# Two layers of linear attention and GELU MLP on one core: the same items in another hand-written order, with f's and y's in longer runs and eleven warming products instead of twelve

## The chip, the cores and the metric

One core of a Trainium2 chip. The metric is the device time of one execution in microseconds, as the median of the runs. The engines are TensorE (PE; its weight loads are PEld), VectorE (DVE), ScalarE (ACT), GpSimd (POOL) and SyncE (SP), which issues nearly all the DMAs.

## The reference

x has 2048 rows of 448 numbers. Two layers are computed, each a linear attention and an MLP, with the same weights in both:

```python
phi = lambda t: jnp.where(t > 0, t + 1, jnp.exp(t)) + 1e-6
def _A_ref(x, wqkv, wo):                      # H = 16 heads of Dh = 28
    q, k, v = ...                             # x @ wqkv, split by heads
    pq, pk = phi(q), phi(k)
    kv = jnp.einsum("bhsd,bhse->bhde", pk, v)
    z = jnp.einsum("bhsd->bhd", pk)
    num = jnp.einsum("bhqd,bhde->bhqe", pq, kv)
    den = jnp.einsum("bhqd,bhd->bhq", pq, z)[..., None] + 1e-6
    return (num / den) @ wo
def _B_ref(x, w1, b1, w2, b2):                # F = 1792
    return gelu(x @ w1 + b1) @ w2 + b2
x = x + _A_ref(layernorm(x), wqkv, wo)
x = x + _B_ref(layernorm(x), w1, b1, w2, b2)  # and both once more
```

## The kernel before

**Tiles and precision.** The 2048 rows are 16 tiles of 128 (t = 0 to 15), in blocks of four. A float32 operand is split into a rounded part and a rest (h and l in the names, for high and low), and a product is three products: high by high, high by low, low by high. Such a split is a cast on ACT (`copy`, L227) for the high part and a subtraction on DVE or POOL for the low one. Since 448 is three pieces of 128 and a tail of 64, the tails of high and low share one piece, so that a product over 448 has 11 matmuls.

**Items.** The whole program is a list of items, two texts in the table `ORDER` (L15 to L118), one for each layer. `run`, at the end of the kernel, goes through a text and calls the function that each item names, with the number behind it as its tile or chunk. A `>` in front of an item means that it belongs to the next layer, so the first text also holds the head of layer 1; a letter behind a colon overrides an engine, a buffer or a bank. Nothing reorders the instructions afterwards: the order of the text is the order in each engine's queue, and each engine works its queue from front to back. An instruction that waits holds up all that is queued behind it on its engine.

**The items that matter here.**

- `hot12` (L240 to L244): twelve products of a 128 x 128 tile of ones with 512 columns of ones, into a bank that nobody reads.
- `ld`, `a`, `ar`, `n`: load of a tile of x on SP; its mean and variance (DVE); the inverse root (POOL); the normalised tile (DVE, or ACT).
- `tu`, `st`, `sp`: a transpose by 32 x 32 squares (DVE), its store and its reload, which put the transposed tile in place; `xh` and `xl` split it (ACT, DVE). In the start-up the transposes are TensorE's instead: `ht`, `hx`, `hl` for tiles 0 and 1, `T` for 2 and 3.
- `K` and `Q` (`proj`, L563 to L567): 11 matmuls of 448 columns each, for one tile. In the start-up the same products are written one matmul at a time, as `hk` and `hq` (L507), in the order in which the pieces of the weights arrive. `wkld`, `wkh`, `wkl`, and the same with q, load and split these weights.
- `ke` and `kp`: phi of K, two passes on ACT and one on DVE. `kh` (ACT, L596) and `kl` (DVE, L600) split it; `za` sums it over the tiles. `qe`, `qp` and `qs` are the same for Q, with a store.
- `sh` (ACT) and `sl` (POOL, L555, L556): the split of the normalised tile as it lies. `G` (L636 to L640): 11 matmuls that add the product of that tile and of phi(K) to four banks.
- `wv`, `wo`: loads of the v and o weights; `woh` and `wol` split the latter. `gt`, `z`, `zb`, `dc` close the sums; `kv` (L709) forms the heads' matrices from the copies of G (`gt`) and the v weights (tile wvt); `m` to `mc` multiply them with wo.
- `pl` to `pT`: the rows of phi(Q) come back, are divided by their denominators and transposed; `o` and `oc` multiply them with the heads' matrices, and `oa` adds the result to x.
- `bld`, `bhi`, `blo`: load (SP), cast (ACT) and subtraction (POOL) of the weights w1 (numbers below 16) and w2 (16 and up), through buffers named xn, W5 and W6; these are the loads called stg from in_B_w_dram.
- `f` (L912 to L917): for a block of four tiles, 11 matmuls of 512 columns that make one chunk of 128 of the 1792 hidden columns. n counts over 14 chunks and 4 blocks, 56 in a layer. `g` is the GELU (ACT, L922), `gh` its cast (ACT, L227), `gl` the low part (DVE, L932).
- `y` (L941 to L944): the chunk's share of the second product, 12 matmuls of 448 columns into four banks. `u` is one of y's four banks alone, written at a block's first chunk. `ya` adds the result to x, `ys` stores it.

**What limits the order.** There are eight banks: four for G and y (`acc`), two for f and Q (`h`), two for K and others (`m`). f(n) takes the bank that g(n−2) has read. The casts gh and the low parts gl have two buffers each (A and B), freed by the y that reads them, and g has three. The start-up buffers xn are two.

Of the kernel before, what the change touches and what calls it, by code (L numbers as in the profile page):

```python
# [16 lines left out]
        "ld0 a0 hot12 ar0 ld1 a1 ar1 wkld1 n0 d0 wkh1 wkld0 ht0 hx0 n1 d1 wkh0 wkl1 ht1 ht2 hl0 wkl0 ld2 wkld2 "  # L17
        "wqld1 wqld0 wkld3 wqld3 ld6 wqld2 ld3 bld4:xn ld4 ld5 hk2 ht3 hk3 hx2 hx1 hl1 wkh2 wqh1 hx3 wqh0 wkl2 "
        "a2 wql1:p wkh3 wqh3 wqh2 hk0 hk8 hk13 hk11 hk14 hk12 hk7 hk4 hk1 hl2 hl3 hq8 hk16 hk9 hq2 hk5 hq7 hq11 "
        "hk18 hq19 hk19 hq3 wkl3 hk10 hk6 wql0 wql3 hk15 hq0 hq1 wql2 hq9 hq10 hq6 hq4 hq5 ar2 ke0 sh0 a3 kp0 n2 "  # L20
        "za0 hq21 hq14 hk17 hq18 hq16 hk20 hq13 hq12 hk21 hq15 hq20 hq17 qe0 kh0 d2 qp0 T2 ar3 sl0 n3 kl0 a5 G0 "
        "ke1 xh2 sh1 ar5 sl1 kp1 xl2 a4 kh1 bld3:xn bhi3 d3 bhi4 qe1 ar4 K2 n5 kl1 n4 tu4 tu5 T3 G1 ld10 qs0 ld9 "
        "ld7 st2 ke2 sh3 qp1 xh3 kp2 a6 za1 a7 xl3 Q2 K3 blo4 sl3 blo3 bld6:xn qs1 ld11 bld2:xn sp2 ar7 ar6 n7 "
        "a9 n6 kh2 sh2 ar9 sl2 kl2 tu6 za2 Q3 bhi2 G2 bhi6 ke3 xh4 tu7 kp3 za3 xh5 kh3 blo2 blo6 ld8 ld14 "
        "bld8:xn st3 bld9:xn xl4 K4 qe3 bhi8 ke4 qe2 xl5 kl3 n9 qp3 K5 Q4 G3 a8 kp4 blo8 ar8 n8 a11 bhi9 kh4 ke5 "
        "sh4 za4 blo9 sl4 ar11 tu9 a14 ar14 kl4 G4 sp3 kp5 xh7 za5 kh5 xh6 bias1:a qs3 bld11:xn ld15 wo0 n14 sh5 "
        "qp2 xl6 tu8 a10 K6 sl5 Q5 qe4 sh6 qp4 n11 kl5 G5 ke6 sl6 ar10 kp6 n10 xl7 bld5:xn bhi5 ld12 st4 qs4 "
        "ld13 sp4 tu14 tu10 tu11 Q7 K7 kh6 bhi11 qe5 xh8 a12 qp5 a13 kl6 blo11 blo5 ar12 za6 ar13 st5 qs2 "
# [12 lines left out]
        "Q13:acc Q12:acc Q14:m mu2 mu3 qe15 qe10 pd5 pz4 pc4 pd4 pm4 pz6 blo24 pc6 qp15 pd6 ld5 ms1 mp0 mp1 yh0 "
        "yh1 bhi25 yl1 pu4 qp10 yl0 yh3 yh2 yl2 yl3 qs15 qs9 bld13:xn qs10 qe13 qe12 bhi13 pl7 pz7 blo13 pc7 pm5 "
        "f0 g0 pu5 gh0 qp13 gl0 pd7 ps2 pm7 pm6 pu6 f1 f2 g1 gh1 qp12 u2 u3 f3 u0 u1 bld19:xn pl9 pz9 pc9 gl1 "
        "pd9 mc2 mc3 qs12 pl8 g2 gh2 g3 pm9 pu9 gl2 y1 gh3 qe11 pz8 qp11 lb3 lb0 pc8 qe14:W6 pd8 gl3 mc0 mc4 "
        "bld21:xn pl10 bhi19 blo19 mc1 pp2 ld7 qs13 lb1 pu7 pz10 blo25 pc10 pd10 bhi21 mc5 ld6 qs11 mc7 pl11 ld9 "
        "bld29:W5 pz11 blo21 mc6 pl13 ps3 bld22:xn pp3 bld23:xn f6 f4 g4 g6 y2 y3 gh4 f5 f9 g5 qh4 bhi22 gh5 "
        "bhi29 gl4 qp14 y4 f7 qh5 gh6 ql4 gl5 g7 ql5 pm8 pm10 oc4 oc5 f8 g9 bhi23 pc11 blo22 blo29 pu10 qh6 ql6 "
        "pu8 gl6 qs14 >wqld0 oa5 oa4 qh7 ps4 bld27:W5 bld26:W6 bhi26 pp4 oc6 y5 y6 gh7 g8 >tab0 gh9 qh8 la4 ar4 "
        "lb2 ln4 pd11 blo23 gl7 la5 ql7 oc7 pz13 pc13 oa6 la6 y7 gl9 qh9 ar6 ln6 ql9 oc9 gh8 gl8 y8 y9 f10 g10 "
        "pm11 mu4 f12 tab1 g12 ar5 blo26 oa7 ln5 f11 mu5 la7 pu11 bld28:W6 pl14 ms2 bhi27 g11 ar7 pd13 oa9 la9 "  # L50
        "ar9 lb6 pl15 ln7 lb7 blo27 mu6 mu7 ql8 mp2 ps5 ms3 pp5 mp3 f13 gh11 pz14 pc14 pd14 gl11 oc8 yh4 g13 "
        "gh10 gl10 y10 y11 yh5 gh12 bhi28 yh7 blo28 gh13 yh6 yl4 yl5 pm13 gl12 yl7 y12 gl13 y13 lb4 pz15 ya0 "
# [960 lines left out]
```

## Time and profile before

| | us |
|---|---|
| median of 3 runs | 870.22 (868.93 to 870.95) |
| the profiled execution | 869.59 |
| its span, from the first to the last recorded instruction | 867.8 |
| PE busy | 860.4 |
| DVE, ACT, POOL busy | 452.7, 356.5, 214.4 |
| the twelve hots, start and length | 1.06, 5.49 |
| start of the first f of layer 0 | 134.05 |
| start of the first f of layer 1 | 561.74 |

A row of the timeline gives the start, the length, the engine and line, the operation, what it writes and reads, the shape, and how many like rows it stands for; in brackets, if the engine was idle before, for how long and what it waited for. A length is that of one matmul through the array; since matmuls overlap, their price is read from one start to the next.

### The profile page before, as it was taken

The numbers are of one execution on the slowest core, as the hardware profiler recorded it, in microseconds if no ns is written. First come the engines' busy times: TensorE is split into PE (matmuls) and PEld (weight loads), VectorE is DVE, ScalarE is ACT, GpSimd is POOL, SyncE is SP. The second block draws the span as 40 slices with busy tenths as digits, with TensorE's granted clock in tenths as the row PEclk, the third lists the DMA queues.
The fourth block names the chain that finished last, engine by engine and source line by source line (L and its number), as shares of the span: only waits on it lengthen the run. The fifth ranks groups of instructions, "written<-read, shape, count | busy, mean of one in ns | idle before, by whom it ended". The sixth has DMA issues, their size and how long they took to land.

```text
span 867.8 us, 11506 instructions
## 1 busy us (share of the span) xinstructions
PE 860.4 (99%) x4144; PEld 767.7 (88%) x4144; DVE 452.7 (52%) x893; ACT 356.5 (41%) x618; POOL 214.4 (25%) x277
## 2 busy tenths in 40 slices
PE   9999999999999999999999999999999999999998
PEld 7999998898888888888899988889888888888887
DVE  7986786575442442235287757846565414332112
ACT  7667646533223313333355664454142332222222
POOL 4655753434110012010123344232222000310000
PEclk9999999999999999999999999999999999999999
DMA  7686367734242113031254634571622402110101
GB/s 223 204 245 188 118 200 214 226 127 131 75 156 71 34 52 119 1 96 50 59 162 155 201 99 130 166 230 40 202 68 99 134 1 88 60 49 1 43 1 42
DMA packets 66393, 98.93 MB, mean 114 GB/s; under 512 B 9249, under 2 KB 60961, under 8 KB 66337
## 3 DMA queue, kind: packets, MB, share of 16 engines
q1 hardware_dynamic: 64528, 98.20, 36.7%
q8 instruction: 32, 0.52, 0.3%
q10 hardware_dynamic: 1808, 0.01, 0.1%
q14 instruction: 25, 0.20, 0.1%
HBM read 58.27 MB, written 36.70 MB: 109 GB/s over the span
## 4 chain that ended last, share of the span: by engine, by line
PE 75%; DMA 3%; DVE 3%; POOL 1%; issue 1%; ACT 1%; SPq 1%; POOLq 0%; ACTq 0%; DVEq 0%
PE y L944 10%; PE y L941 10%; PE y L942 10%; PE hp L912 8%; PE hp L913 8%; PE hp L916 8%; PE op L847 3%; PE hp L914 3%; PE hp L917 3%; PE op L850 2%; PE psk L563 1%; PE psq L563 1%; DMA sp<-sq_m 1%; PE G L636 1%; PE G L638 1%
## 5 line engine op out<-in xcount | busy, mean ns | idle before, releaser
L932 DVE TENSOR_TENSOR gl<-g,gh 128x512 fp32r<-128x512 f32 x112 | 78.0, 704 | 257.6 <-ACT gh L227 229.4
L922 ACT ACTIVATE g<-hp,b1s 128x512 f32<-128x512 f32 x112 | 76.7, 688 | 324.6 <-PE hp L917 311.8
L941 PE MATMUL y<-w2h,gh 128*128 128x448 f32 x448 | 162.4, 362 | 0.0
L942 PE MATMUL y<-w2l,gh 128*128 128x448 f32 x448 | 162.1, 362 | 0.0
L912 PE MATMUL hp<-XH,w1h 128*128 128x512 f32 x336 | 131.5, 391 | 1.1 <-ACT XH L227 0.7
L913 PE MATMUL hp<-XH,w1l 128*128 128x512 f32 x336 | 131.5, 391 | 0.0
L373 POOL TENSOR_TENSOR brs<-bmv,mhalf 128x1 f32<-128x1 f32 x64 | 37.1, 583 | 328.3 <-DVE bmv L367 323.3
L944 PE MATMUL y<-w2h,gl 128*128 128x448 f32 x448 | 115.7, 362 | 0.0
L916 PE MATMUL hp<-XL,w1h 128*128 128x512 f32 x336 | 94.4, 389 | 0.0
L941 PEld LDWEIGHTS y<-w2h,gh 128*128 128x128 f32 x448 | 84.0, 187 | 7.5
L942 PEld LDWEIGHTS y<-w2l,gh 128*128 128x128 f32 x448 | 84.0, 188 | 7.3
L227 ACT CAST gh<-g 128x512 fp32r<-128x512 f32 x112 | 68.4, 619 | 53.5 <-PE y L942 46.4
L944 PEld LDWEIGHTS y<-w2h,gl 128*128 128x128 f32 x448 | 83.9, 188 | 5.5
L912 PEld LDWEIGHTS hp<-XH,w1h 128*128 128x128 f32 x336 | 63.0, 188 | 13.8 <-ACT XH L227 1.5
L916 PEld LDWEIGHTS hp<-XL,w1h 128*128 128x128 f32 x336 | 63.1, 188 | 13.2
L913 PEld LDWEIGHTS hp<-XH,w1l 128*128 128x128 f32 x336 | 63.1, 188 | 12.1
L776 POOL TENSOR_TENSOR pz<-pq,zb 128x448 f32<-128x448 f32 x32 | 38.2, 1193 | 87.4 <-DMA pq<-pq_d 34.2
L448 DVE TENSOR_TENSOR XL<-sp,XH 128x512 fp32r<-128x512 f32 x60 | 42.8, 725 | 32.2 <-ACT XH L227 32.0
L876 POOL TENSOR_TENSOR x<-x,b2b 128x448 f32<-128x448 f32 x32 | 39.5, 1244 | 44.7 <-DVE xm L381 44.7
L555 POOL TENSOR_TENSOR xnl<-x,xnh 128x384 fp32r<-128x384 f32 x32 | 33.2, 1038 | 53.1 <-ACT xnh L227 37.1
L914 PE MATMUL hp<-XH,w1x 128*128 128x512 f32 x112 | 43.6, 389 | 0.0
L917 PE MATMUL hp<-XL,w1x 128*128 128x512 f32 x112 | 43.6, 389 | 0.0
(167 smaller groups left out, 1415.1 us busy)
## 6 DMA issues: line engine op xcount, KB each, us to landing
sq_m<-sq SPq DMA_DIRECT2D x16, 512.0 KB, 3.0
sp<-sq_m SPq DMA_DIRECT2D x64, 128.0 KB, 3.3
x<-in_A_x_dram SPq DMA_DIRECT2D x32, 224.0 KB, 3.3
pq_d<-eq SPq DMA_DIRECT2D x32, 224.0 KB, 3.3
sq_a<-sq SPq DMA_DIRECT2D x14, 512.0 KB, 3.6
sp<-sq_a SPq DMA_DIRECT2D x56, 128.0 KB, 3.2
pq<-pq_d SPq DMA_DIRECT2D x32, 224.0 KB, 2.9
x<-x_d SPq DMA_DIRECT2D x32, 224.0 KB, 3.1
```

The source lines that it names most:

```text
L227: act.copy(out, src)
L448: dve.tensor_sub(squares(lo), spread_tile(kind, l, t), f(squares(hi)))
L912: pe.matmul(o, w1h[:, c, s], x.moving(x.hi, c), start=(c == 0), stop=False)
L913: pe.matmul(o, w1l[:, c, s], x.moving(x.hi, c), start=False, stop=False)
L914: pe.matmul(o, w1x[:, s], x.moving(x.hi, 3), start=False, stop=False)
L916: pe.matmul(o, w1h[:, c, s], x.moving(x.lo, c), start=False, stop=False)
L917: pe.matmul(o, w1x[:, s], x.moving(x.lo, 3), start=False, stop=True)
L922: act.activation(T[l, "g", n], T[l, "hp", n], AF.Gelu_apprx_tanh, bias=b1s[:, n % NF:n % NF + 1])
L932: dve.tensor_sub(lo, T[l, "g", n], f(hi))
L941: pe.matmul(o, gh[:, r], w2h[:, i], start=first, stop=False)
L942: pe.matmul(o, gh[:, r], w2l[:, i], start=False, stop=False)
L944: pe.matmul(o, gl[:, r], w2h[:, i], start=False, stop=last)
```

## The change

Only the table `ORDER` changes. Both texts have the same items as before, except that `hot12` is now `hot11` and stands in front of the first loads, and that 33 items of layer 1 which stood at the head of the second text (among them K3, G1, G2, Q2, Q3, with their splits, and ld8, ld11) now stand at the end of the first, while ld12 goes the other way. Numbers of lines behind the table grow by one. The diff replaces all lines of the table; a few of each text:

```diff
-        "ld0 a0 hot12 ar0 ld1 a1 ar1 wkld1 n0 d0 wkh1 wkld0 ht0 hx0 n1 d1 wkh0 wkl1 ht1 ht2 hl0 wkl0 ld2 wkld2 "
+        "hot11 ld0 a0 ar0 ld1 a1 ar1 wkld1 n0 d0 wkh1 wkld0 ht0 hx0 n1 d1 wkh0 wkl1 ht1 ht2 hl0 wkl0 wkld2 wqld1 "
...
-        "hk18 hq19 hk19 hq3 wkl3 hk10 hk6 wql0 wql3 hk15 hq0 hq1 wql2 hq9 hq10 hq6 hq4 hq5 ar2 ke0 sh0 a3 kp0 n2 "
-        "za0 hq21 hq14 hk17 hq18 hq16 hk20 hq13 hq12 hk21 hq15 hq20 hq17 qe0 kh0 d2 qp0 T2 ar3 sl0 n3 kl0 a5 G0 "
+        "hq11 hq0 hq13 hq7 wkl3 wql0 wql3 wql2 hk13 hq3 hk18 hk6 hk10 hq1 hk21 hq9 hq6 hq4 hq10 hq5 hq15 hq21 "
+        "ar2 ke0 sh0 a3 n2 kp0 za0 hq19 hk19 hq12 hq14 hq18 hk20 hq16 hq20 hq17 hk17 hk15 qe0 d2 kh0 sh1 qp0 T2 "
...
-        "G10 st7 kp11 za10 xl13 K12 sp7 ld1 qs8 wo1 wv2 wv1 wv3 xh14 kh11 woh1 sh11 xh15 ke12 za11 xl14 kl11 "
+        "sh9 woh0 qe5 sh10 ke10 kp10 st7 sp7 qs6 xh14 kh10 kl10 za10 sl9 sl10 wol0 G9 wv1 sp6 ld7 wv0 wo1 wv3 "
+        "G10 ke11 xh13 xh12 sh11 kp11 xl12 xl13 K12 sh12 kh11 xh15 ke12 qp5 za11 kl11 kp12 xl14 sl11 G11 K13 "
+        "kh12 sh14 qe8 za12 kl12 K14 ke13 woh1 sl12 sl14 G12 kp13 xl15 kh13 ke14 sh13 wol1 sl13 kl13 za13 kp14 "
```

Three places show what moves in the engines' queues. The first is TensorE's queue in the MLP of layer 1, chunks 22 to 27 (hp is an f's bank, y0 to y3 the banks of a y; the numbers tell tiles apart). Before:

```order
L944 MATMUL y2_6500<-w2h_107,gl_6743 128x448
L944 MATMUL y3_6526<-w2h_107,gl_6743 128x448
L912 MATMUL hp_6839<-XH_6287,w1h_103 128x512
L913 MATMUL hp_6839<-XH_6287,w1l_104 128x512
L912 MATMUL hp_6839<-XH_6287,w1h_103 128x512
L913 MATMUL hp_6839<-XH_6287,w1l_104 128x512
L912 MATMUL hp_6839<-XH_6287,w1h_103 128x512
L913 MATMUL hp_6839<-XH_6287,w1l_104 128x512
L914 MATMUL hp_6839<-XH_6287,w1x_105 128x512
L916 MATMUL hp_6839<-XL_6288,w1h_103 128x512 x3
L917 MATMUL hp_6839<-XL_6288,w1x_105 128x512
L941 MATMUL y0_6522<-w2h_107,gh_6858 128x448
```

And now (the last rows of f24, then f22, then the first of f25):

```order
L917 MATMUL hp_6744<-XL_6197,w1h_103 128x512 x3
L918 MATMUL hp_6744<-XL_6197,w1x_105 128x512
L913 MATMUL hp_6761<-XH_6196,w1h_103 128x512
L914 MATMUL hp_6761<-XH_6196,w1l_104 128x512
L913 MATMUL hp_6761<-XH_6196,w1h_103 128x512
L914 MATMUL hp_6761<-XH_6196,w1l_104 128x512
L913 MATMUL hp_6761<-XH_6196,w1h_103 128x512
L914 MATMUL hp_6761<-XH_6196,w1l_104 128x512
L915 MATMUL hp_6761<-XH_6196,w1x_105 128x512
L917 MATMUL hp_6761<-XL_6197,w1h_103 128x512 x3
L918 MATMUL hp_6761<-XL_6197,w1x_105 128x512
L913 MATMUL hp_6789<-XH_6196,w1h_103 128x512
```

Before, f27 stood alone between y22 and y23. Now f24, f22, f25, f27 and f26 run one behind the other, and y22 to y25 follow together.

The second place is SP's queue in layer 1, from the load of wo's second half (wot) to the last load of v weights (wvt; x_5 and the like are tiles of x, pq the returning rows of phi(Q)). Before:

```order
L656 DMA wot<-in_A_wo_dram 112x2x448
L648 DMA wvt<-in_A_wqkv_dram 128x448 x2
L650 DMA wvt<-in_A_wqkv_dram 64x448
L651 DMA wvt<-in_A_wqkv_dram 64x448
L770 DMA pq_0_5179<-pq_d_78 128x448
L455 DMA x_5_5181<-x_d_79 128x448
L770 DMA pq_1_5183<-pq_d_78 128x448
L455 DMA x_0_5185<-x_d_79 128x448
L455 DMA x_2_5187<-x_d_79 128x448
L770 DMA pq_2_5189<-pq_d_78 128x448
L648 DMA wvt<-in_A_wqkv_dram 128x448
```

And now:

```order
L657 DMA wot<-in_A_wo_dram 112x2x448
L651 DMA wvt<-in_A_wqkv_dram 64x448
L652 DMA wvt<-in_A_wqkv_dram 64x448
L456 DMA x_3_5171<-x_d_79 128x448
L771 DMA pq_0_5173<-pq_d_78 128x448
L626 DMA pq_d_78<-eq 128x448 x2
L771 DMA pq_2_5178<-pq_d_78 128x448
L456 DMA x_8_5180<-x_d_79 128x448
L456 DMA x_4_5182<-x_d_79 128x448
L771 DMA pq_1_5184<-pq_d_78 128x448
L456 DMA x_0_5186<-x_d_79 128x448
L649 DMA wvt<-in_A_wqkv_dram 128x448
```

Before, all but one of the wvt loads stood ahead of pq_0, and the last was the seventh row from pq_0 on. Now two wvt loads stand ahead of wot, and the last is the eighth row and ninth load from pq_0 on (two stores of Q's phi, in one row, are in front of it).

The third place is ACT's queue in layer 0, at the cast of the w1 load number 9 (the last cast to w1h in each piece; ek and eq are the two passes of phi for a K and a Q tile, XH the cast of a transposed tile). Before:

```order
L574 ACTIVATE ek<-ek 128x448
L227 CAST XH<-sp 128x512 x2
L596 ACTIVATE kh<-psk,tiny 128x448
L573 ACTIVATE eq<-psq 128x448
L574 ACTIVATE eq<-eq 128x448
L227 CAST w1h<-stg 128x448
L573 ACTIVATE ek<-psk 128x448
L574 ACTIVATE ek<-ek 128x448
L573 ACTIVATE eq<-psq 128x448
L574 ACTIVATE eq<-eq 128x448
L227 CAST w1h<-stg 128x448
L596 ACTIVATE kh<-psk,tiny 128x448
```

And now:

```order
L597 ACTIVATE kh<-psk,tiny 128x448
L228 CAST w1h<-stg 128x448
L574 ACTIVATE eq<-psq 128x448
L575 ACTIVATE eq<-eq 128x448
L228 CAST XH<-sp 128x512
L574 ACTIVATE ek<-psk 128x448
L575 ACTIVATE ek<-ek 128x448
L228 CAST w1h<-stg 128x448
L574 ACTIVATE eq<-psq 128x448
L575 ACTIVATE eq<-eq 128x448
L228 CAST w1h<-stg 128x448
L597 ACTIVATE kh<-psk,tiny 128x448
```

Before, the casts bhi2 and bhi6 stood ahead of these rows, and bhi8 and bhi9 in them. Now bhi6, bhi2 and bhi9 stand in this order between kh3 and kh4. bhi9's load goes to the buffer that blo6, a subtraction on POOL behind bhi6, sets free.

185 rows, old and new, of the table ORDER are left out of this document.

## The prediction

> **What bounds the kernel now.** I read the page's busy line first, then the busy time by windows, then TensorE's waits, and only then single stretches of the timeline.
>
> ```profile
> PE 860.4 (99%) x4144; PEld 767.7 (88%) x4144; DVE 452.7 (52%) x893; ACT 356.5 (41%) x618; POOL 214.4 (25%) x277
> ```
>
> TensorE is busy 99% of the 867.8 us span, and no other engine comes near. In the table by windows (start and end, length, then the busy time of PE, PEld, DVE, ACT and POOL) I compare PE with the length.
>
> ```profile
> 20.00:100.00 80.00, 79.97 (x401) 74.26 (x400) 62.98 (x126) 58.35 (x114) 49.65 (x60) 1.00 0.68 207
> 150.00:430.00 280.00, 280.00 (x1321) 247.51 (x1320) 118.97 (x227) 94.82 (x157) 51.94 (x57) 1.00 0.31 94
> 500.00:590.00 90.00, 88.37 (x448) 78.73 (x447) 57.52 (x113) 48.16 (x82) 31.86 (x41) 1.00 0.54 160
> ```
>
> In the MLP of layer 0 nothing is lost; the attention of layer 1 (500 to 590) loses 1.6 us; and from 20 to 100 DVE and ACT are busy three quarters of the time, so a queue there has little slack. The granted clock is 1.00 throughout. TensorE's waits (total, times, longest) are few:
>
> ```profile
> PE hot L244 <- POOL ones L182: 1.1, 1, 1.1
> PE hp L912 <- ACT XH L227: 0.7, 2, 0.4
> PE kvp L709 <- DMA wvt<-in_A_wqkv_dram: 0.5, 1, 0.5
> PE psk L563 <- DVE kl L600: 0.4, 1, 0.4
> PE psq L563 <- DVE eq L578: 0.4, 1, 0.4
> PE hp L912 <- ACT g L922: 0.4, 1, 0.4
> PE psQ L507 <- ACT wq L227: 0.2, 1, 0.2
> ```
>
> They sum to 3.7 us. The matmul count changes by one, so the change can win only from these few waits, from the start-up, or from the price of a matmul itself. That price is not quite constant:
>
> ```profile
> 817.40 0.39 PE L912 MATMUL hp<-XH,w1h 128*128 128x512 f32 x1
> 819.92 0.39 PE L912 MATMUL hp<-XH,w1h 128*128 128x512 f32 x1
> 822.41 0.39 PE L912 MATMUL hp<-XH,w1h 128*128 128x512 f32 x1
> 824.91 0.37 PE L941 MATMUL y<-w2h,gh 128*128 128x448 f32 x1
> 829.72 0.39 PE L912 MATMUL hp<-XH,w1h 128*128 128x512 f32 x1
> ```
>
> Three f's in a row, then two y's, from start to start. The first f, behind a y, takes 2.52 us; the second and third, behind an f, 2.49 and 2.50. The two y's take 4.81 us, 0.200 for each of 24 matmuls. Counted over the whole timeline, 62 f's stand behind a y, and all but 10 take 2.52 or more; 43 stand behind an f, and all but one take 2.49.
>
> **The change part by part.** Durations are of one profiled execution, 869.59 us with 1.8 us outside its span; it lies 0.63 below the median of 870.22. The sum is a difference, and I apply it to the median.
>
> *Bursts.* f's that start behind a y or an attention product fall from 69 to 26: 43 of them lose the step from 2.52 to 2.49. At 0.025 to 0.03 each, that is 1.1 to 1.3 us; without the one f in six that shows no step it is 0.9, and the y's begun behind an f, also 43 fewer, may gain some ns each. Nothing hides it, for the windows show PE full. I take −1.3 (−0.9 to −1.4).
>
> The Trainium skill, "TensorE: Matmul & The Clock Gate", section "Wait — 56ns, not 53.3ns?", states that warm matmuls start N/2.4 GHz plus about 2.5 ns apart, by width alone. By that the bursts would bring nothing; the 2.52 against 2.49 above speaks against it, and its 189 ns at N = 448 stands against a measured 200.
>
> *Eleven hots, and the start-up.*
>
> ```profile
> 1.06 5.49 PE L244 MATMUL hot<-ones 128*128 128x512 f32 x12 [1.06 <-POOL ones L182]
> 6.44 0.57 ACT L227 CAST wk<-stg 128x448 fp32r<-128x448 f32 x1 [0.55 <-DMA stg<-in_A_wqkv_dram]
> 7.01 0.37 ACT L227 CAST XH<-tp 128x256 fp32r<-128x256 f32 x1
> 7.44 0.47 PE L507 MATMUL psK<-wk,XH 128*128 128x448 f32 x1
> 10.01 1.15 POOL L311 TENSOR_TENSOR wq<-stg,wq 128x448 fp32r<-128x448 f32 x1 [4.04 <-ACT wq L227]
> 13.20 1.03 ACT L227 CAST wq<-stg 64x448 fp32r<-64x448 f32 x2
> 14.14 0.53 ACT L573 ACTIVATE ek<-psK 128x448 f32<-128x448 f32 x1
> 14.28 0.68 PE L507 MATMUL psQ<-wq,XL 128*128 128x448 f32 x2 [0.24 <-ACT wq L227]
> 14.70 0.58 ACT L574 ACTIVATE ek<-ek 128x448 f32<-128x448 f32 x1
> 17.80 0.49 PE L410 MATMUL tp<-ident,x 128*128 128x128 f32 x3
> ```
>
> One hot is worth 0.46 us (5.49 over 12). But the first product at 7.44 waits for ACT's cast of XH (7.01), which stands behind the cast of a weight that landed at 6.44, and at 14.28 TensorE waits for the last wq cast of a row of ACT casts. Neither moves with the hots. Behind that cast 17 matmuls were left before T2 at 17.80, by the new table 18: +0.2 (−0.46 to +0.6, three matmuls).
>
> The same page, Part 1 "The HAM clock gate", states that the clock goes up by windows of time, about 3.4 us, not by a count of matmuls; here the hots, 0.46 apart against 0.23 between the f's matmuls, ran at half speed for 5.5 us.
>
> *Layer 0's K and G products.* ACT and DVE work in queues, and loads of w1 stand in them.
>
> ```profile
> 30.72 1.03 ACT L227 CAST w1h<-stg 128x448 fp32r<-128x448 f32 x2 [4.44 <-DMA stg<-in_B_w_dram]
> 33.54 0.77 PE L640 MATMUL G<-kh,xnl 128*128 128x448 f32 x3
> 33.66 1.14 ACT L227 CAST XH<-sp 128x512 fp32r<-128x512 f32 x2 [0.85 <-DMA sp<-sq_a]
> 34.34 1.48 PE L563 MATMUL psk<-wk,XH 128*128 128x448 f32 x6
> ```
>
> ACT waits 4.44 us for a load, and PE loses 0.2 of it (33.54 + 3 × 0.200 = 34.14; the next starts at 34.34). Now bhi6, bhi2 and bhi9 come close together on ACT. bhi9's buffer is that of bld6, freed by blo6 on POOL:
>
> ```profile
> L555 POOL TENSOR_TENSOR xnl<-x,xnh 128x384 fp32r<-128x384 f32 x32 | 33.2, 1038 | 53.1 <-ACT xnh L227 37.1
> stg<-in_B_w_dram SPq DMA_DIRECT2D x26, 224.0 KB, 3.4
> ```
>
> From the end of bhi6: sl3 1.04, blo6 about 1.15 (the like subtraction at 10.01), the load 3.4, together 5.6 us. ACT has 4.4 us between: three pairs of Relu and Exp at 1.11, XH 0.57, w1h 0.52. So ACT waits some 1.2 us in front of kh4. G4, which needs kh4, stands 44 matmuls (8.8 us) behind K4, and that covers it. I count three such places at 0.2, +0.6; the ends are −0.2 (the old loss gone) and +1.5 (bhi9's wait and a bit of kh4's own chain uncovered).
>
> *Layer boundary.* psq's 0.4 in the waits lies where K0 to K3 and Q0 to Q3 get a new order and some thirty items of layer 1's first pass (K3, G1, G2, Q2, Q3 and the casts, subtractions and loads that belong to them) move ahead of ys13, the last store of layer 0. On SP, ys13 now comes behind st3, qs3 and ld11, and ld13, which reads what it stored, comes a few rows later; behind ld13 stands qs2, and a13, which needs it, has G3, K5, K4, Q4 and Q7 ahead, 55 matmuls or 11 us. POOL gets sl2 and sl3 earlier, in front of sl6. So the stores cost nothing, and the one wait may go or come again elsewhere: −0.3 (−0.8, as a stall can cost twice its wait, see the next, to +0.6).
>
> *wo's second half, layer 1.*
>
> ```profile
> 502.92 0.33 SPq L656 DMA_DIRECT2D wot<-in_A_wo_dram  x1
> 508.52 0.94 ACT L227 CAST woh<-wot 112x896 fp32r<-112x896 f32 x1 [2.92 <-DMA wot<-in_A_wo_dram]
> 511.08 1.21 PE L636 MATMUL G<-kh,xnh 128*128 128x448 f32 x4
> 514.08 1.47 PE L563 MATMUL psk<-wk,XH 128*128 128x448 f32 x6 [0.39 <-DVE kl L600]
> ```
>
> ACT waits 2.92 us for a load issued 5.6 earlier; sh11, xh15 and ke12 queue behind it. G's 11 matmuls from 511.08 should end at 513.28; the next K starts at 514.08, 0.8 late. The new table puts G10, K12, G11, K13 and K14 (55 matmuls, 11 us) between load and cast, so that stall goes. What is late next is K14's own chain, which the old table ran without a wait: −0.8 (−0.9 to 0).
>
> *kv in layer 1.*
>
> ```profile
> 523.19 0.37 SPq L648 DMA_DIRECT2D wvt<-in_A_wqkv_dram  x1
> 528.45 3.37 PE L709 MATMUL kvp<-gt,wvt 128*112 128x112 f32 x32 [0.50 <-DMA wvt<-in_A_wqkv_dram]
> ```
>
> The last wvt is issued at 523.19 and ends TensorE's wait 5.26 us later. It was the seventh DMA of a run on SP's queue from pl0 on, and is now the ninth; two more issues at 0.4 delay it by up to 0.8, and it is last to arrive already: +0.4 (0 to +0.8).
>
> *f's behind f's.* Their number doubles, 43 to 86. f(n) needs the h bank that g(n−2) frees.
>
> ```profile
> 581.48 0.69 ACT L922 ACTIVATE g<-hp,b1s 128x512 f32<-128x512 f32 x1 [4.43 <-DMA pq_d<-eq]
> 582.22 0.50 PE L912 MATMUL hp<-XH,w1h 128*128 128x512 f32 x1 [0.37 <-ACT g L922]
> ```
>
> One of the 43 stalled, behind a g of 0.69 against an f of 2.49. A g may be 1.8 us late at no cost, and the burst's gh's stay two deep, as their rings do. One more stall of 0.4 to 0.8 is +0.3 once its chance is counted (−0.6 to +1.3). The two f0 waits (0.7 in all) and the tail have the same work ahead: 0 (±0.6).
>
> Sum: −1.3 + 0.2 + 0.6 − 0.3 − 0.8 + 0.4 + 0.3 = −0.9, so 868.7 for a run like the profiled one and 869.3 for the median. About 0.2%, 1.74 us, is what a measurement of this kernel can tell from no change.
>
> **The rivals.** (a) Faster: the small stalls all go, and layer 0 costs nothing: −1.3 − 0.8 − 0.8 (boundary) − 0.6 (582) + 0 = −3.5, 866.7. For it: each stall sits behind one awkwardly placed wait. Against: a new order brings new places of its own.
>
> (b) Slower, by loads in ACT's queue: if bhi9's load comes as late as the one at 30.72 (4.44 us) while kh4's cover is used up by the waits of bhi6 and bhi2, PE loses the 4.44 nearly whole: −0.9 + 4.4 = +3.5, 873.7. It decides as soon as new waits uncover 2.6 us. For it: 62.98 and 58.35 busy of 80. Against: PE lost 0.2 of 4.44 last time.
>
> (c) Slower, by the h banks: if one in five of the 43 new f's behind f's stalls as at 582.22, with 0.6 each, 9 × 0.6 = 5.4 − 0.9 − 0.3 = +4.2, 874.4. Against: 1 in 43 so far.
>
> (d) No burst gain: if the 0.025 comes with something else that a y is followed by, such as the h bank's change of hands, and not with the switch itself, longer bursts keep it: −0.9 + 1.3 = +0.4, 870.6. Against it stand the 62 and the 43 f's above. The same time would come out by the Trainium skill's rule of spacing by width alone (the page and section above).
>
> (e) The clock goes up later for want of a hot: the eight matmuls or so from 7.44 at half speed, 8 × 0.2 = +1.6, of which ACT's casts hide part: −0.9 + 1.6 = +0.7, 870.9.
>
> That the table does not do what it says is out: the order of TensorE's rows shows the bursts.
>
> **How the numbers follow.** Forecast 0.37, (a) 0.34, (b) 0.13, (c) 0.07, (d) 0.06, (e) 0.03. Faster is (a), 0.34; same is the forecast, (d) and (e), 0.46; slower is (b) and (c), 0.20. The likeliest case's own range is 868.5 to 871.9. The range given takes in (a) with 0.7 below it for the open ends of layer 0 and the start, and above goes to 872.8, which leaves out (b) and (c) at their full price.
>
> **What would show it.** In the profile after: f behind f still 2.49; no wait of ACT for wot in layer 1 and no 0.8 us gap there; T2 at about 18.0; the last wvt still TensorE's wait before kv; waits of hp for g at most two. I am wrong if f's behind f's wait for g, if PE in 20 to 100 loses over 1 us, or if f's cost 2.52 wherever they stand.

## The result, and the profile after

The changed kernel took 876.81 us in the median of 6 runs (876.36 to 880.36), the kernel before 870.96 (6 runs, 868.93 to 871.68): a ratio of 1.008, 95% interval 1.006 to 1.010. It is slower by 0.8%, where 869.3 was forecast, with 872.8 as the upper end. The profiled execution took 876.36, its span 874.6, 6.8 more than before.

The busy line of the page after, and the table by windows for the same three stretches:

```profile
PE 861.4 (98%) x4143; PEld 768.5 (88%) x4143; DVE 461.7 (53%) x893; ACT 359.5 (41%) x620; POOL 220.1 (25%) x277
```

```profile
20.00:100.00 80.00, 78.58 (x394) 72.94 (x393) 64.22 (x126) 56.47 (x108) 49.25 (x57) 1.00 0.69 198
150.00:430.00 280.00, 279.56 (x1320) 247.21 (x1319) 127.49 (x232) 95.72 (x157) 52.93 (x57) 1.00 0.32 95
500.00:590.00 90.00, 86.48 (x434) 77.93 (x433) 58.20 (x114) 46.27 (x79) 32.58 (x41) 0.98 0.55 160
```

TensorE now loses 1.4 us from 20 to 100, where it had lost nothing, and 3.5 instead of 1.6 from 500 to 590; there the granted clock is 0.98. Its waits after:

```profile
PE hp L913 <- ACT g L923: 1.9, 3, 0.8
PE kvp L710 <- DMA wvt<-in_A_wqkv_dram: 1.7, 1, 1.7
PE psk L564 <- ACT XH L228: 1.4, 1, 1.4
PE hp L913 <- ACT XH L228: 1.2, 2, 0.7
PE psk L567 <- DVE XL L449: 0.6, 1, 0.6
```

To see where all of the 6.8 us is, I add up, from the start of each matmul to the start of the next, the time of each kind of product. A wait counts with the product ahead of it.

| from start to start, us | before | after | |
|---|---|---|---|
| start-up: hots, first transposes, psK, psQ | 17.5 | 17.7 | +0.2 |
| K (psk) | 66.2 | 68.9 | +2.7 |
| G | 72.4 | 71.2 | −1.2 |
| z and kv of both layers | 7.7 | 11.1 | +3.4 |
| Q, m, o, oc, transposes | 148.2 | 148.4 | +0.2 |
| f (hp) | 281.7 | 283.2 | +1.5 |
| y | 269.1 | 269.0 | −0.1 |

Three places carry it: kv of layer 1, one K of layer 0, and the first f's of the two MLPs. G's −1.2 is for the most part two waits of the kernel before, of the psq at 453.75 and of the psk at 514.08, which count with the G ahead of them.

**kv of layer 1.** SyncE's issues and TensorE's rows after:

```profile
523.98 0.33 SPq L771 DMA_DIRECT2D pq<-pq_d  x1
524.73 2.10 SPq L626 DMA_DIRECT2D pq_d<-eq  x2
529.33 0.37 SPq L649 DMA_DIRECT2D wvt<-in_A_wqkv_dram  x1
530.99 0.37 PE L685 MATMUL zp<-zh,ones 128*128 128x448 f32 x1
531.39 0.79 PE L710 MATMUL kvp<-gt,wvt 128*112 128x112 f32 x4
533.91 4.59 PE L710 MATMUL kvp<-gt,wvt 128*112 128x112 f32 x28 [1.72 <-DMA wvt<-in_A_wqkv_dram]
538.27 1.46 PE L564 MATMUL psq<-wq,XH 128*128 128x448 f32 x6
```

The last wvt goes out 5.35 us after pl0 (the first row) instead of 2.81. Before, the first row of this run was:

```profile
520.38 0.33 SPq L770 DMA_DIRECT2D pq<-pq_d  x1
```

The two stores of phi(Q) in between took SyncE 2.10 us, and 1.4 of that is the second one's wait for a pass of VectorE, by the list of the waits of SP's queue:

```profile
SPq L626 <- DVE psk L579: 1.4, 1, 1.4
```

TensorE's wait is 1.7, but kv lasts 6.9, from 531.39 to 538.27. The rest is the clock:

```profile
534.00:536.00 2.00, 2.00 (x14) 2.00 (x15) 1.35 (x3) 0.00 (x0) 2.00 (x3) 0.64 0.00 0
536.00:538.00 2.00, 2.00 (x13) 2.00 (x12) 0.00 (x0) 0.00 (x0) 0.72 (x2) 0.50 0.00 0
```

The column behind POOL's is the granted clock. It is half of full speed from shortly after the wait until 538.

**K14 of layer 0.** SyncE's queue, then ACT's and TensorE's rows, after:

```profile
71.04 0.43 SPq L257 DMA_DIRECT2D b2b<-in_B_b_dram  x1
71.52 0.43 SPq L456 DMA_DIRECT2D x<-in_A_x_dram  x1
72.05 0.38 SPq L657 DMA_DIRECT2D wot<-in_A_wo_dram  x1
72.47 0.93 SPq L456 DMA_DIRECT2D x<-in_A_x_dram  x2
73.44 2.95 SPq L431 DMA_DIRECT2D sp<-sq_a  x4
83.86 0.57 ACT L228 CAST w1h<-stg 128x448 fp32r<-128x448 f32 x1 [2.24 <-DMA stg<-in_B_w_dram]
86.10 0.61 ACT L228 CAST XH<-sp 128x512 fp32r<-128x512 f32 x1
86.77 1.48 PE L564 MATMUL psk<-wk,XH 128*128 128x448 f32 x6 [1.42 <-ACT XH L228]
```

ACT stands 2.24 us at the load of bhi1 (83.86). xh14 (86.10) is four casts behind it, and K14 waits for xh14. Before, a single load stood just ahead of sp7, and the two casts waited for nothing:

```profile
69.73 0.43 SPq L648 DMA_DIRECT2D wvt<-in_A_wqkv_dram  x1
72.98 2.61 SPq L430 DMA_DIRECT2D sp<-sq_a  x4
80.15 0.55 ACT L227 CAST w1h<-stg 128x448 fp32r<-128x448 f32 x1
80.61 0.61 ACT L227 CAST XH<-sp 128x512 fp32r<-128x512 f32 x1
```

Now SyncE is held up too. It issued the load of bhi1 only at 79.05, after the load of wo had landed at 78.99:

```profile
SPq L263 <- DMA wot<-in_A_wo_dram: 1.3, 1, 1.3
```

In none of the fourteen profiles of this case are more than eight of SyncE's transfers under way at the end of an issue; with eight under way, the next issue came only after one had landed. Whether the chip or the program sets that number, no run shows.

**The first f's.** ACT's and TensorE's rows at the beginning of layer 1's MLP, after:

```profile
572.57 1.28 ACT L923 ACT_TABLE_LOAD   x1 [2.04 <-DVE eq L579]
573.86 0.69 ACT L923 ACTIVATE g<-hp,b1s 128x512 f32<-128x512 f32 x1
574.60 0.50 PE L913 MATMUL hp<-XH,w1h 128*128 128x512 f32 x1 [0.84 <-ACT g L923]
```

The first g waits until 572.57 for the buffer that it writes (the bracket names a VectorE pass that ended then; the store that reads this buffer landed at 572.48), then for its table, and starts at 573.86; the third f waits for the bank that this g reads. Layer 0 has two waits of an f for a g, at 142.2 and 157.8.

Later in the MLP the bursts do as they should. Three f's behind a y in layer 1:

```profile
831.59 0.39 PE L913 MATMUL hp<-XH,w1h 128*128 128x512 f32 x1
834.11 0.39 PE L913 MATMUL hp<-XH,w1h 128*128 128x512 f32 x1
836.60 0.39 PE L913 MATMUL hp<-XH,w1h 128*128 128x512 f32 x1
839.09 0.37 PE L942 MATMUL y<-w2h,gh 128*128 128x448 f32 x1
```

The first takes 2.52 us, the second and third 2.49 each. Over the whole timeline 54 f's behind a y or an attention product, and without a wait, had the step before; 19 have it now.

### The profile page after: what moved, and what is told of

Its sections match the earlier page's. It is cut to its first block, busy times and chain, and to the rows that moved or that the text cites. A ratio compares the mean times of both kernels' runs of the same rounds, so it can differ in the third digit from the quotient of the medians.

```text
span 874.6 us, 11478 instructions
## 1 busy us (share of the span) xinstructions
PE 861.4 (98%) x4143; PEld 768.5 (88%) x4143; DVE 461.7 (53%) x893; ACT 359.5 (41%) x620; POOL 220.1 (25%) x277
## 4 chain that ended last, share of the span: by engine, by line
PE 82%; DMA 6%; DVE 5%; ACT 3%; SPq 2%; issue 1%; POOL 1%; ACTq 0%; DVEq 0%; POOLq 0%
PE y L942 10%; PE y L945 10%; PE y L943 10%; PE hp L913 8%; PE hp L914 8%; PE hp L917 8%; PE op L848 3%; PE hp L915 3%; PE hp L918 3%; PE psk L564 2%; PE psq L564 2%; PE op L851 2%; PE G L639 1%; PE psk L567 1%; PE G L637 1%
## 5 line engine op out<-in xcount | busy, mean ns | idle before, releaser
L449 DVE TENSOR_TENSOR XL<-sp,XH 128x512 fp32r<-128x512 f32 x60 | 45.6, 773 | 34.0 <-ACT XH L228 34.0
L228 ACT CAST XH<-sp 128x512 fp32r<-128x512 f32 x60 | 35.7, 615 | 19.2 <-DMA sp<-sq_a 9.8
```

The costliest lines, as they stand in the source:

```text
L228: act.copy(out, src)
L449: dve.tensor_sub(squares(lo), spread_tile(kind, l, t), f(squares(hi)))
```

## The experiments

The theory now: the bursts are sound; the time is lost where the new table puts a DMA further back on SyncE, or its consumer nearer, than the old one. The rivals: the losses belong to the bursts, or the DMA engines are simply too busy and any order waits. In the edits the lines are pieces of the two texts.

**a_wv2**: one swap in layer 1.

```diff
-sp6 ld7 wv0
+sp6 wv2 wv0
...
-ld0 wv2 G14
+ld0 ld7 G14
```

> The changed kernel with one swap in layer 1: the last load of v weights (wv2) takes the place of the load of x's tile 7 behind sp6, some 15 us earlier, and ld7 goes where wv2 stood. Theory: kv's 10.3 us (before: 6.2) come from that load alone, a wait of 1.9 us and, as its consequence, half the granted clock for the 3.6 us after it; both go, kv takes 6.2 to 6.4 us again, the granted clock is 1.00 throughout, and the time falls by 4.0 us to about 872.8. Rival 1: the load is late because the DMA engines are busy there, and whatever is loaded last waits; then kv still waits over 1 us and the time falls by less than 1.5. Rival 2: the half clock belongs to that stretch of the program and not to the wait; then the wait goes (1.9) and the slow matmuls stay (2.2).

Measured: 875.16 (872.16 to 877.09, 10 runs). The wait at kv is gone, and so is the half clock. TensorE's rows and the windows of this run:

```profile
533.70 3.67 PE L710 MATMUL kvp<-gt,wvt 128*112 128x112 f32 x32
537.14 1.46 PE L564 MATMUL psq<-wq,XH 128*128 128x448 f32 x6
```

```profile
88.50:92.50 4.00, 4.00 (x12) 3.61 (x13) 2.44 (x4) 2.55 (x5) 4.00 (x6) 0.57 0.26 68
530.00:540.00 10.00, 10.00 (x68) 9.23 (x67) 7.34 (x14) 2.79 (x6) 4.78 (x8) 1.00 0.62 196
```

kv takes 3.4 us (533.70 to 537.14) instead of 6.9, at a clock of 1.00 (second row). Both rivals fall, for this place. The median fell by 1.7 only, not by 4.0: in this profile K14 waited 3.1 us instead of 1.6, and the half clock stands behind that wait (first row). The mean granted clock, which is on record for each run, tells the runs apart: the four at 1.000 took 872.16 to 874.33, around the 872.8 expected, and the six at 0.996 to 0.998 took 875.11 to 877.09. Where the clock fell in the runs without a profile is not shown.

**a_xh14**: one move in layer 0.

```diff
-kh12 bhi1 woh0 sh12 sh13 xh14 bhi20
+kh12 xh14 bhi1 woh0 sh12 sh13 bhi20
```

> The changed kernel with one move in layer 0: the cast xh14 goes in front of bhi1, woh0, sh12 and sh13 on ScalarE. Theory: K14's wait of 1.6 us at 86.8 comes from ScalarE standing 2.2 us at bhi1's load with xh14 queued behind it; the wait goes and the time falls by 1.6 us to about 875.2. Rival: xh14 is late by its own reload, or the wait only moves on to the next product behind these casts (K15 or G12); then the time falls by less than 0.5.

Measured: 874.68 (872.30 to 878.47, 7 runs); the profiled run is the longest of them. K14's wait is gone, but K15 waits 1.2 us for kl13, which needs kh13, which is behind the same loads. The rival holds in part: what moves is the place of the wait. In this run the kv wait was 2.8.

**a_start**: three moves at the beginnings of the MLPs.

```diff
-qs10 bld13:xn pl7 bld29:W5 qs13 ld7
+qs10 qs13 bld13:xn pl7 bld29:W5 ld7
...
-bhi21 g5
+g5 bhi21
...
-mc4 pl8 qs9 mc2 pl7 qs12
+qs9 mc4 qs12 pl8 mc2 pl7
```

> The changed kernel with three moves at the beginnings of the two MLPs: on SP the stores qs13 (layer 0) and qs9 and qs12 (layer 1) go ahead of loads, so that the buffers that the first two GELUs write come free earlier; on ScalarE bhi21 goes behind g5. Theory: the three waits of an f for a g (0.8 at 142.2, 0.6 at 157.8, 1.0 at 574.6) come from these, not from the bursts; they go, and the time falls by 2.4 to 2.8 us to about 874.2. Rival: an f run that long must wait for its two banks anyway, and the waits turn up at the next f's; then f's total stays at 283.2 us and the time within 0.8.

Measured: 876.53 (872.68 to 878.54, 6 runs); the profiled run is again the longest. f's total fell from 283.2 to 280.8, as the theory has it; the bursts don't force these waits. But y's rose by 1.2, since y's now wait for gh, and K's by 2.3, with a wait of 2.6 at K14 and half the clock behind it, a place that this edit does not touch. The time stayed.

**a_all**: the three together.

> All the moves of the other three together. Theory: they are independent, the sum of the falls is 8.0 to 8.4 us, and the time is about 868.6, faster than both kernels: what is then left of the change is its gain from the bursts, 0.8 us, and from wo's load. Rival: the waits overlap or hand on what they save, and the time stays above the 870.9 of the kernel before.

Measured: 871.90 (870.62 to 875.51, 12 runs), ratio to before 1.0024 (1.0010 to 1.0038). Five of the 5.9 us are back, not eight. In the profiled run (874.96) layer 0 still waits, 1.5 at K15 and 0.7 at a G, and an f waits 1.3 at 161. SyncE's row for the reload sp7 and ACT's for xh14 in this run told the next cause:

```profile
73.82 3.13 SPq L431 DMA_DIRECT2D sp<-sq_a  x4
84.81 0.62 ACT L228 CAST XH<-sp 128x512 fp32r<-128x512 f32 x1 [2.82 <-DMA sp<-sq_a]
```

Now xh14 waits for its own reload sp7, whose four parts landed 8.1 to 8.8 us after their issue; the like took 3.2 in the median before. Ahead of it on SyncE stand the five loads that the profile of the changed kernel shows above (four rows, one of them for two loads), 1288 KB.

**a_bulk**: these five behind sp7 and bld1 instead.

```diff
-bld12:xn bias2 ld1 wo0 ld5 ke11
+bld12:xn ke11
...
-blo12 ld2 sp7 qs7 bld1:xn bld20:xn
+blo12 sp7 qs7 bld1:xn bias2 ld1 wo0 ld5 ld2 bld20:xn
...
-kh12 bhi1 woh0 sh12
+kh12 bhi1 sh12
...
-kh13 kl13 xl15 K14
+kh13 woh0 kl13 xl15 K14
```

> The changed kernel with SyncE's queue in layer 0 mended: the five loads that stand just ahead of the reload sp7 (bias2, ld1, wo0, ld5, ld2: 1.29 MB in all) go behind bld1; woh0, which needs wo0, goes behind kh13 on ScalarE. Theory: xh14 and bhi1 came late because sp7 and bld1 stood behind these loads in the DMA queue (1.29 MB at the 230 GB/s of that stretch are 5.6 us); sp7 lands within 4 us of its issue, ScalarE waits less than 1 us before bhi1, K14's wait at 87 goes, and K's total falls from 68.9 to 67.3 us or less: 1.6 us of time, 3 and more in executions where half the clock followed. Rival: it is ScalarE's order alone (bhi1 too close behind bld1, whenever that lands); then the wait stays over 1 us.

Measured: 876.69 (876.12 to 878.11, 4 runs), the time of the changed kernel. ACT's and TensorE's rows:

```profile
81.20 0.56 ACT L228 CAST w1h<-stg 128x448 fp32r<-128x448 f32 x1
82.79 0.61 ACT L228 CAST XH<-sp 128x512 fp32r<-128x512 f32 x1
87.23 0.57 ACT L228 CAST w2h<-stg 128x448 fp32r<-128x448 f32 x1 [3.82 <-DMA stg<-in_B_w_dram]
91.56 1.48 PE L564 MATMUL psk<-wk,XH 128*128 128x448 f32 x6 [2.12 <-DVE kl L601]
```

sp7's four parts landed 3.6 to 4.0 us after their issue, bhi1 (81.20) and xh14 (82.79) wait for nothing, and K14's wait is gone: that part of the theory holds. But bld20 now stands behind the five loads, and its cast bhi20 (87.23) waits 3.8 us in front of kh13; K15 pays 2.3. It is the same stop, moved one cast on, and the time does not fall as expected.

**a_all2**: a_bulk, a_wv2 and a_start, and qh4 and qh5 behind g4.

```diff
-pp2 qh4 pu7 pz9 pc9 ql4 pd9 qs11 mc1 qh5 g4
+pp2 pu7 pz9 pc9 pd9 qs11 mc1 g4 qh4 ql4 qh5
```

> The moves of a_bulk, a_wv2 and a_start together, with qh4 and qh5 behind g4 on ScalarE in layer 0. Theory: the four places where a product waits for a transfer that SyncE issues late are gone; against the 870.9 of the kernel before there are left the start-up (+0.2), the two f0's (+0.4), two waits of the head of layer 1 (+0.5), and the bursts' gain (0.8): about 870.5 to 871.0, no difference that can be told. Rival: the waits are handed on from place to place, as with xh14; then it stays at 872 to 873.

Measured: 874.49 (874.01 to 875.92, 5 runs). K15 waits 2.5, a y 1.9 at 180 for a gh behind a late weight load, where before there was none; f's total is 280.5, the lowest of all. The rival holds, and more than it says: the waits are handed on, and the time is over its 872 to 873.

**a_all3**: a_bulk, a_wv2 and the two store moves of a_start; and bhi20, the cast that then stood in the way, is moved away from its load.

```diff
-xh14 bhi20 K13
+xh14 K13
...
-sl13 blo20 wol1
+sl13 wol1
...
-kh14 bhi16 G13
+kh14 bhi20 bhi16 blo20 G13
```

> a_bulk, a_wv2 and the two store moves of a_start together (bhi21 stays where the change put it), and bhi20 with its blo20 behind kh14, away from its load. Theory: with the load's cast out of kh13's way, K15's wait (2.3 in a_bulk, 2.5 in a_all2) goes too, no wait in layer 0's attention is over 0.6 us, and the time is 869.5 to 870.5, level with the kernel before or a little under. Rival: the loads are simply too many for that stretch, the wait turns up at the next cast of a load (bhi16, or woh0), and the time stays at 872 or more.

Measured: 869.86 (868.55 to 870.53, 12 runs) beside 870.74 of the kernel before (23 runs): ratio 0.9983 (0.9972 to 0.9995). Waits left over, of 0.8 us and more in total:

```profile
PE hp L913 <- ACT XH L228: 1.3, 2, 0.7
PE hp L913 <- ACT g L923: 1.2, 2, 1.0
PE hot L245 <- POOL ones L183: 1.1, 1, 1.1
PE G L637 <- POOL xnh L557: 0.8, 1, 0.8
```

No K in layer 0 waits any more; one G's wait of 0.95 (start to start) is over the 0.6 expected, and the time is inside the range expected. So the new order is as good as the old one and a little better, once its late transfers are put right. Whether the bursts make it better is another question, which the next run bears on.

**b_best**: the kernel before with its own three waits of layer 1 mended, no bursts.

```diff
-sp7 ld1 qs8 wo1
+sp7 wv0 qs8 wo1
...
-pl2 wv0 G14
+pl2 ld1 G14
...
-kh11 woh1 sh11
+kh11 sh11
...
-kp12 qp5 kh12 za12
+kp12 qp5 kh12 woh1 za12
...
-u0 mc3 pl9 pz9 pc9 pd9 ld4 mc6 qs15 mc2
+u0 qs15 mc3 pl9 pz9 pc9 pd9 ld4 mc6 mc2
```

> The kernel before with its own three waits in layer 1 mended and no bursts: the last load of v weights changes places with the load of x's tile 1 on SyncE; woh1 goes behind kh12 on ScalarE, 5 us after its load's wait; the store qs15 goes ahead of mc3. Theory: the waits at kv (0.5), at K14 (0.8) and of f for g (0.6) go, nothing else moves, and the time falls by 1.5 to 2.0 us to about 868.5 to 869. Rival: as in the changed kernel, what is gained at one place is waited for at the next, and the time stays at 870 to 871.

Measured: 869.49 (867.96 to 870.91, 12 runs), ratio 0.9982 (0.9972 to 0.9993). The waits at kv and K14 are gone; the f's wait for g at 580 is 1.15 instead of 0.5, and an o waits 1.2 for qh. Both theories have a share: 1.3 of the 1.5 to 2.0. The old order with its own waits mended is thus as fast as a_all3 with its bursts (869.49 and 869.86). f's total in a_all3 is 282.3 against 281.7 before: the waits that are left there stand against what the bursts save, and a gain of the bursts in the time of the whole kernel is not shown.

**b_wv0**: the kernel before with two transfers more ahead of its last wvt.

```diff
-pl2 wv0 G14
+pl2 pl3 qs5 wv0 G14
...
-ld3 qs5 ld8 pl3 pz3
+ld3 ld8 pz3
```

> The kernel before with two transfers more (pl3 and qs5) ahead of its last load of v weights on SyncE, as many as the prediction counted. Theory: two more issues at 0.4 us delay the load by 0.8, kv takes 7.0 us instead of 6.2, and the clock stays at 1.00, since a wait of 1.5 us is too short to lower it. Rival: a store that stands between can hold SyncE for longer than its issue (in the changed kernel one took 1.7 us), and kv takes 8 us or more.

Measured: one run, 870.75. wvt was issued at 524.29 instead of 523.19, and z and kv of both layers took 8.2 instead of 7.7: +0.5, at full clock. So two transfers that are ready, a load and a store, cost about what the prediction had counted, in one run. It was not their number that made the difference.

**b_hot11**: the kernel before with one hot fewer.

```diff
-ld0 a0 hot12 ar0
+ld0 a0 hot11 ar0
```

> The kernel before with eleven hots instead of twelve and nothing else. Theory: TensorE's transposes begin 0.43 us earlier and what follows does not, since ScalarE's casts of the weights set its pace; hot, tp, psK and psQ together take 17.5 us from start to start as before, within 0.5, and the clock is up by the first K product. Rival: one hot fewer leaves the first eight products at half the clock, 1.6 us.

Measured: one run, 869.08. The start-up's sum is 16.9 instead of 17.5; over the profiles here it lies between 16.4 and 18.5, so one hot can't be told from it. psK and psQ take 10.2 together, as before: the rival falls. The hots keep their place behind ld0 here, so that moving them ahead of the first load is not tried apart.

**micro**: a tail that computes nothing of use, behind the kernel before.

```diff
+    for run_, total in ((1, 12), (2, 12), (4, 12), (1, 12)):
+        for r in range(total // run_):
+            for i in range(run_):
+                ff(hs[i % 2], i)
+            for i in range(run_):
+                yy(os, i)
...
+    for k in (1, 2, 3, 4, 5, 6, 8):
...
+        pe.matmul(gm, w1h[:, 0, :128], xs.hi[:, :512], start=True, stop=True)
...
+        act.copy(gt_, gm)
+        for j in range(k - 1):
+            act.copy(gt_, f(gt_))
+        pe.matmul(hs[0], gt_[:, :128], xs.hi[:, :512], start=True, stop=True)
+        for r in range(6):
+            ff(hs[r % 2], r)
```

`ff` is 11 matmuls of 512 columns, `yy` 12 of 448.

> The kernel before with a tail that computes nothing of use: 12 f-like and 12 y-like products (11 matmuls of 512 and 12 of 448 columns) taking turns by 1, by 2, by 4 and by 1 again; then by 1 with f's moving data read as one plain run of 512 instead of four pieces of 128; then TensorE kept waiting behind 1, 2, 3, 4, 5, 6 and 8 passes of ScalarE over 512 columns (some 0.6 us each), with 66 matmuls of 512 columns after each wait. Theory of the bursts: an f behind a y takes 2.52 us, an f behind an f 2.49, so 12 pairs by turns cost 0.3 us more than by fours. Rival: all f's take the same. Theory of the clock: after a wait of up to 1.6 us the matmuls after it start 0.227 us apart, after a wait of 2.6 us and more they start 0.427 apart for some 3 to 4 us, and in between it depends on the place. Rival: the clock falls only after a wait of 3.4 us or more, as windows of that length would have it if a window had to be idle altogether.

Measured, from start to start:

| | f | y |
|---|---|---|
| by turns | 2.518 | 2.408 |
| twos, each two | 5.012 | 4.808 |
| fours, each four | 9.998 | 9.608 |
| by turns, f's data in one plain run | 2.518 | 2.408 |

An f behind an f is 5.012 − 2.518 = 2.494. The step is 0.025 for an f and 0.008 for a y, and goes with the switch, not with how f's data is read. Of the waits, those of 0.8 to 2.8 us left the clock alone, those of 3.4, 4.1 and 5.4 lowered it: the rival's picture, but with one wait of each length.

**micro2**: waits of three lengths, three times each, behind f-like and kv-like products.

```diff
+    for kind in (0, 1):
+        for k in (2, 3, 4, 2, 3, 4, 2, 3, 4):
+            if kind:
+                kk(1)
...
+            if kind:
+                kk(15, gt_)
+            else:
+                pe.matmul(hs[0], gt_[:, :128], xs.hi[:, :512], start=True, stop=True)
```

The wait between is made as in micro; `kk(n)` is n float32 products of 112 columns.

> The kernel before with another tail that computes nothing of use. TensorE waits behind 2, 3 and 4 passes of ScalarE (1.5, 2.1 and 2.8 us), three times each; once with f-like products of 512 columns before and behind the wait, and once with a kv-like product (float32, 112 columns, four passes each) before it and fifteen behind it. Theory: what lowers the clock is how little TensorE works within a stretch of some 3.4 us, and kv's short matmuls, whose weights load before each, count for less than f's: behind the f-like products no wait of this length lowers the clock, behind the kv-like ones the waits of 2.1 and 2.8 us do in most cases (the short matmuls start 0.187 us apart instead of 0.098). Rival: only the wait's length and its place against the chip's windows count; then both kinds show the same.

Measured, times that the clock fell to half:

| wait | f-like | kv-like |
|---|---|---|
| 1.5 to 1.6 us | 0 of 3 | 0 of 3 |
| 2.1 to 2.2 us | 1 of 3 | 2 of 3 |
| 2.8 to 2.9 us | 2 of 3 | 2 of 3 |

Behind waits of over 2 us these are three of six against four of six: no difference that can be told. The rival holds: what counts is the wait's length, and where it falls; the last section has that from the traces.

## Why the prediction was wrong

**The step that failed first: "kv in layer 1, +0.4 (0 to +0.8)".** It was +3.4 for z and kv. The prediction counted two more DMAs at 0.4 us. b_wv0 shows that this price was right for transfers that are ready. In the new order one of the two stores was not: it waited 1.4 us for VectorE, the two took SyncE 2.1 us, and the load left 2.5 us later relative to pl0. The wait that came of it was then long enough to bring down the clock, which cost about as much again: 6.9 us for a kv that takes 3.4 in a_wv2 and took 3.1 before. a_wv2 removed both by one swap. The prediction had no clock at all in this term. Rival (e) spoke of it, but only for the start.

**"Layer 0's K and G products, +0.6 (−0.2 to +1.5)"** was low: K14's wait alone is 1.6, and 2.6 and 3.1 in the profiles of two kernels with the same layer-0 attention (a_start, a_wv2), with half the clock behind it. The mechanism is rival (b)'s, a load's cast in front of casts that TensorE needs, but not at bhi9, which the prediction worked out; no K waits there. It was bhi1, where the prediction did not look: five bulk loads had come ahead of sp7 and bld1. Here the late transfers could not be read from ACT's queue alone. a_bulk shows that the five loads were the reason (sp7's parts landed 3.6 to 4.0 us after their issue instead of 6.9 to 7.9), a_all3 that the casts' distance from their loads is what has to be kept.

**"f's behind f's, +0.3 (−0.6 to +1.3)"** was low as well: three waits, 2.4 in all, against 0.5 before. They are not rival (c)'s, spread over the bursts; of the 86 f's behind an f only these three waited. a_start took them away at their causes (a store late, a load's cast ahead of a g) with the bursts left as they were.

**"Bursts, −1.3 (−0.9 to −1.4)"**: right in kind, at the lower end in size, 35 steps of 0.025 or 0.9. The Trainium skill's rule of spacing by width alone ("TensorE: Matmul & The Clock Gate", "Wait — 56ns, not 53.3ns?") does not show here: micro has 2.518 and 2.494 for the same eleven matmuls. Rival (d) falls. That nothing hides the gain, as the prediction has it, is not shown: in the time of the whole kernel it is not to be seen (a_all3 beside b_best).

**"Layer boundary, −0.3"** came out at about +0.3: psq's wait (0.5 beyond the usual step) went, and a K at 478.9 waits 0.8 for its XL. **"wo's second half, −0.8"**: woh1's wait went, as forecast, but a wait of 0.4 for kl at 514.07, inside a G, took its place; net −0.4. **The start-up, +0.2**: +0.2, T2 at 18.04 as forecast; but this sum lies between 16.4 and 18.5 over the profiles, so that the agreement in size may be luck.

The common fault: every step was priced by the queue that it stands in, at the pace of before. Six of the seven terms came out worse than forecast and none better. Two of the signs of being wrong that the prediction had named came: f's behind f's wait for g, and PE loses 1.4 us from 20 to 100.

What stays open: the load of bhi1 landed 4.8 us after its issue in the changed kernel's profile and 5.4 and 5.7 in those of a_start and a_wv2, and K14 waited 1.6, 2.6 and 3.1; why the same transfers take so differently long is not shown. Nor is it shown what the runs between 876.4 and 880.4 differ in, since only one of each kernel is profiled; the longest has a mean granted clock of 0.993 where the other five have 0.998, so that more half clock is a part of it.

## What to carry to other kernels

With the bound engine at 99%, a new order gains in hundredths per item and loses in microseconds per late transfer, so look first at each queue of DMAs: what stands ahead of the transfer that is needed next, in bytes, in transfers under way and in stores that must wait themselves, and how much work lies between a load and the cast that reads it. A queue that works in order hands its wait on, and mending one place (a_xh14, a_bulk) can bring nothing until the whole chain behind it has been mended (a_all3). A wait of the matrix engine of some 2 us can cost nearly twice its length: behind it came 3.41 us at half the clock, which is 1.7 us of work lost.

## What the runs showed of the hardware

Half the granted clock followed waits much shorter than I had thought of. Waits of up to 1.6 us never lowered it; waits of 1.9 to 3.1 us did in some cases and not in others (the kv waits of 1.9, 2.2, 2.6 and 2.8 and the K14 waits of 2.6 and 3.1 did, the K15 waits of 2.3 and 2.5 and the y's wait of 1.9 and micro's of 2.1 and 2.8 did not, and in micro2 seven of twelve did), and the three of 3.4 and more in micro all did. It then stayed down for 3.41 us each time, and for 6.83 behind the waits of 4.1 and 5.4.

What decides is how much of a wait falls into one window of time. In each of the seven traces with more than one stretch at half clock (a stretch behind the last matmul counts too), the stretches begin whole multiples of 3.413 us apart. That gives each execution a grid of windows. Two waits of the same length in micro2, each with the windows that it lies in and, in the last row, the window after the second wait:

```profile
892.54:895.95 3.41, 2.04 (x10) 1.34 (x8) 0.00 (x0) 1.27 (x3) 0.00 (x0) 1.00 0.00 0
895.95:899.37 3.42, 2.82 (x12) 2.36 (x13) 0.00 (x0) 0.55 (x1) 0.00 (x0) 1.00 0.03 5
991.53:994.94 3.41, 1.44 (x6) 0.86 (x5) 0.00 (x0) 1.82 (x3) 0.00 (x0) 1.00 0.00 0
994.94:998.35 3.41, 3.41 (x9) 2.63 (x8) 0.00 (x0) 0.00 (x0) 0.00 (x0) 0.50 0.00 0
```

The first wait, 1.97 us by the profile's idle times, is shared by two windows, 1.4 and 0.6, and the clock stays at 1.00. The second lies whole in one window, and the next window runs at 0.50. Over all fourteen profiles, from the first matmul to the last, TensorE's idle time sorts the windows nearly without exception: behind all 15 that had 1.9 us or more of it the clock was half, behind none of the 23 that had 1.0 to 1.5, and behind one of the 7 in between, with 1.7 to 1.86 (kv of the changed kernel, 1.72). The K15 waits of a_bulk and a_all2 were shared in this way (1.74 and 0.38, 1.25 and 1.09). The Trainium skill ("TensorE: Matmul & The Clock Gate", Part 1, "The HAM clock gate") has windows of 3.4 us that run freely, and a clock that falls after an idle one; the grid agrees with the windows, but here 1.9 us idle of 3.41 were enough. The rule was read from the traces afterwards; no run was made to test it.

A reload of 512 KB in four parts, issued behind 1288 KB of other loads, landed 8.1 to 8.8 us after its issues (a_all), where 3.2 is the median before; with those loads behind it, after 3.6 to 4.0 (a_bulk). And a product of 512 columns that follows one of 448 costs 0.025 us more, one of 448 that follows 512 0.008 (micro).
